# A sparse-attention and gated feed-forward kernel: unit 1's neighbour keys moved to where their transposes have landed, and part of its small copies given to ScalarE

## Chip, cores, metric

One core of a Trainium2 chip (the kernels ran on different chips, with the kernel before beside each). The metric is the device time of one execution in microseconds (us); each kernel's number is the median of its runs. Engines are named as in the profile: PE (matmul), PEld (weight load), DVE (VectorE), ACT (ScalarE), POOL (GpSimd), SP (SyncE).

## The reference, cut to what matters

```python
# attention, q,k,v: (4, 8, 768, 64) f32; block 32, window 16
k_sum = k.reshape(B,H,24,32,64).max(axis=3)       # a key per block: maximum over its 32 keys
v_sum = v.reshape(B,H,24,32,64).mean(axis=3)      # a value per block
# softmax over [local keys with |i-j| < 16] and [24 block keys, + log 32], times [v ; v_sum]
# then, on x = attention output as (3072, 512):
ffn = (gelu(x @ w_gate) * (x @ w_val)) @ w_out    # 512 -> 1536 -> 512
out = x + sigmoid(x @ w_res) * ffn
```

## The kernel before

The work is cut into eight units: unit u is half of batch u // 2, 384 tokens. While PE does the feed-forward of unit u, the attention of unit u + 1 is threaded in between. For one unit PE does twelve "columns" (line 398: four matmuls for the gate, g, and four for the value, vv), then in the tail scores (s, L330), residual gates (r, L416), the output matmuls (f, L432), attention outputs (ao, L362) and transposes (xp, L381). Each engine works in order through its own list of instructions: in the trace of before, the product gvT of column 9 could have run at about 66.03 us and ran at 67.73, behind work that waited for a DMA.

Unit 1 is special: it prepares batch 1, whose first use comes with unit 2. For each pair of heads a tile kW holds 64 own keys a row tile, their 16 neighbours on either side, and the 24 block keys; own keys of pairs 2 and 3 arrive by transposing DMAs. The value tile vext is loaded in even rows of tiles only; the odd ones are copied ("spread") from them, and block means are broadcast into rows 96 to 127.

```python
ps_mm = ...tile_pool(name="ps_mm", bufs=4, space=PSUM)   # results of matmuls; g, vv, r, f share four banks
...
def fo_end(gvT, fo, g, vv):
    nc.scalar.activation(ge[:], g[:, 0:TU], AF.Gelu)          # ACT; frees g's bank
    nc.vector.tensor_mul(gvT[:, fo, :], ge[:], vv[:, 0:TU])   # DVE; frees vv's bank
...
def k_rest(kw, copy=nc.vector.tensor_copy):
    nc.vector.tensor_max(km[:], ...)                          # L209
    nc.vector.tensor_reduce(out=ks..., in_=km[:], op=ALU.max) # L211, block keys
    copy(kw[:, 1:NT, 0:WIN], ...)                             # L213, neighbours before
    copy(kw[:, 0:NT - 1, POST:POST + WIN], ...)               # L214, neighbours after
    nc.vector.tensor_copy(kw[:, :, BLK0:BLK0 + NB], ...)      # L215, block keys
...
def v_spread(b, c0, c1, part):                                # part 0: L291, part 1: L294
def vsum_bc(b, hp, lo, hi, mul=...):                          # L300 for batches 0 and 1
...
# unit 1, after its columns 8 and 11
if u == 1 and fo in (8, FO - 1):
    k_rest(kW[1][2 if fo == 8 else 3])
...
# unit 1's tail
s_step(n, 0, nst); s_step(n, 1, nst, two=(AO, TT))            # scores, exponentials, masks
res_step(st, 0)
ffn_step(st, gvT, 0, 0, FO)
if u == 1:
    v_spread(1, 0, HT // 2, 0)
    v_spread(1, 0, HT // 2, 1)
    end_step(u, st, 0)                                        # two DVE ops on f
    vs = vsum_sum(1, *SS, last=True)                          # PE: block means
    vsum_out(1, vs, 0, H, nc.scalar.copy)
    for hp in range(NP):
        vsum_bc(1, hp, 0, HT)
res_step(st, 1)
if u == 1:
    ffn_step(st, gvT, 1, 0, 6)
# AO, TT, MM, SS name places in PSUM; rz: 1 / row sum, xn: normalised output
av_step(n, 0, nst, *AO); av_step(n, 1, nst, *TT)              # PE: ao; DVE: rz (L370), xn (L372)
s_step(n, 2, nst); s_step(n, 3, nst, two=(MM, MM), masked=False)
...                                                           # xp needs xn
```

The softmax here doesn't subtract the row's maximum and nothing guards it: scores larger than these inputs give would overflow.

Of the kernel before, what the change touches and what calls it, by code (L numbers as in the profile page):

```python
# [15 lines left out]
def kernel(  # L16
# [11 lines left out]
    nc = tc.nc  # L28
    B, H, S, D = q.shape
# [8 lines left out]
    FO = DFF // 128  # L38
    QT = 64
    NT = S // QT  # L40
    HT = NT // 2
# [3 lines left out]
    NP = H // 2  # L45
# [27 lines left out]
    kW = [[const.tile([128, NT, 128], BF16, name=f"kW{i}_{p}") for p in range(NP)] for i in range(2)]  # L73
# [30 lines left out]
    with tc.manual_schedule():  # L104

        def vext_consts(i):
            nc.vector.memset(vext[i][:, :, :, D:D + 1], 1.0)
            nc.vector.memset(vext[i][0:WIN, 0], 0.0)
            nc.vector.memset(vext[i][64:96, NT - 1], 0.0)
            nc.vector.memset(vext[i][64:64 + WIN, NT - 1, :, D:D + 1], 1.0)  # L110
# [57 lines left out]
        def gate(t):  # L168
            nc.gpsimd.tensor_copy(tick[:], t)
# [36 lines left out]
        def k_rest(kw, copy=nc.vector.tensor_copy):  # L206
            own = kw[:, :, OWN:OWN + QT].rearrange("d t (n w) -> d t n w", w=BLK)
            km = work.tile([128, NT, 2, BLK // 2], BF16, tag="km", name="km")
            nc.vector.tensor_max(km[:], own[:, :, :, 0:BLK // 2], own[:, :, :, BLK // 2:BLK])  # L209
            ks = work.tile([128, NB], BF16, tag="ks", name="ks")  # L210
            nc.vector.tensor_reduce(out=ks.rearrange("d (t n) -> d t n", n=2), in_=km[:],  # L211
                                    axis=mybir.AxisListType.X, op=ALU.max)
            copy(kw[:, 1:NT, 0:WIN], kw[:, 0:NT - 1, OWN + QT - WIN:OWN + QT])  # L213
            copy(kw[:, 0:NT - 1, POST:POST + WIN], kw[:, 1:NT, OWN:OWN + WIN])  # L214
            nc.vector.tensor_copy(kw[:, :, BLK0:BLK0 + NB], ks.unsqueeze(1).to_broadcast([128, NT, NB]))  # L215
# [68 lines left out]
            copy(vsum[b % 2][96:128, h0:h1, 0:D],  # L284
                 vs[96:128, h0 * D:h1 * D].rearrange("p (h d) -> p h d", d=D))

        def v_spread(b, c0, c1, part):

            V = vext[b % 2].rearrange("p (c e) h d -> p c e h d", e=2)
            if part == 0:  # L290
                nc.vector.tensor_copy(V[0:64, c0:c1, 1, :, 0:D], V[64:128, c0:c1, 0, :, 0:D])  # L291
            else:
                hi = min(c1, NC - 1)
                nc.vector.tensor_copy(V[64:96, c0:hi, 1, :, 0:D], V[0:32, c0 + 1:hi + 1, 0, :, 0:D])  # L294

        def vsum_bc(b, hp, lo, hi, mul=nc.vector.tensor_scalar_mul):
            dst = vext[b % 2][96:128, lo:hi, 2 * hp:2 * hp + 2, 0:D]
            if b < 2:
                src = vsum[b][96:128, 2 * hp:2 * hp + 2, 0:D]
                nc.vector.tensor_copy(dst, src.unsqueeze(1).to_broadcast([32, hi - lo, 2, D]))  # L300
            else:
                src = vsB[96:128, hp].rearrange("p (h d) -> p h d", d=D)
                mul(dst, src.unsqueeze(1).to_broadcast([32, hi - lo, 2, D]), 1.0 / BLK)
# [89 lines left out]
        def half_fo(st, w, fo, lo, hi, acc=None):  # L393
            fs = slice(fo * 128, (fo + 1) * 128)
            if acc is None:
                acc = ps_mm.tile([128, 512], F32, tag="mm", name="g" if w is w_gate else "vv")
            for ko in range(lo, hi):
                nc.tensor.matmul(acc[:, 0:TU], w[:, ko, fs], st["xT"][:, ko, :],  # L398
                                 start=(ko == 0), stop=(ko == KO - 1))
            return acc  # L400

        def fo_end(gvT, fo, g, vv):
            ge = work.tile([128, TU], F32, tag="ge", name="ge")
            nc.scalar.activation(ge[:], g[:, 0:TU], AF.Gelu)  # L404
            nc.vector.tensor_mul(gvT[:, fo, :], ge[:], vv[:, 0:TU])  # L405

        def fo_step(st, gvT, fo):
            g = half_fo(st, w_gate, fo, 0, KO)
            vv = half_fo(st, w_val, fo, 0, KO)
            fo_end(gvT, fo, g, vv)  # L410
# [16 lines left out]
        def ffn_step(st, gvT, sub, lo, hi, c0=0, c1=DM):  # L427
            ss = slice(sub * 128, (sub + 1) * 128)
            if lo == 0:
                st["f", sub] = ps_mm.tile([128, 512], F32, tag="mm", name="f")  # L430
            for fo in range(lo, hi):
                nc.tensor.matmul(st["f", sub][:, 0:c1 - c0], gvT[:, fo, ss], w_out[:, fo, c0:c1],  # L432
                                 start=(fo == 0), stop=(fo == FO - 1))
# [17 lines left out]
        def values_step(u, fo):  # L451

            b = u // 2 + 1
            if u in (2, 4) and fo >= FO - NP:
                block_sums(vT[b], fo - FO + NP)
            if u in (3, 5):
                if fo in (1, 3):
                    v_spread(b, 0, HT // 2, fo // 2)
                if 6 <= fo < 10:
                    vsum_bc(b, fo - 6, 0, HT, nc.scalar.mul)  # L460
            if u % 2 == 0 and u < NU - 1:
                if fo in (0, 1):
                    v_spread(b - 1, HT // 2, NC, fo)
                if 2 <= fo < 2 + NP:
                    vsum_bc(b - 1, fo - 2, HT, NT)
# [66 lines left out]
        for u in range(NU):  # L532
            b, half = u // 2, u % 2
# [16 lines left out]
            for fo in range(FO):  # L550
                if u == 0 and fo < 2:
                    for w, _, acc in firsts[2 * fo:2 * fo + 2]:
                        half_fo(st, w, fo, KO - 1, KO, acc)
                    fo_end(gvT, fo, firsts[2 * fo][2], firsts[2 * fo + 1][2])
                elif u > 3 and fo == 0:
                    fo_end(gvT, fo, firsts[0][2], firsts[1][2])
                elif u > 3 and fo == 1:
                    fo_end(gvT, fo, firsts[2][2], half_fo(st, w_val, fo, 0, KO))
                else:
                    fo_step(st, gvT, fo)  # L560
                values_step(u, fo)
                if u == 0 and fo == 4:
                    nc.vector.memset(vsT[:], 0.0)
                    load_rows(1)
                if u == 0 and fo == 6:
                    vext_consts(1)
                if u == 0 and fo == FO - 1:
                    kw_consts(1)
                    for c in range(NC + 1):
                        load_values(1, c)  # L570
                if u == 2 and fo == FO - 1:
                    gate(gvT[0:1, fo, 0:1])
                    load_rows(3)
                if half == 0 and 1 < nb < B and fo == 0:
                    vT[nb] = turn_values(nb)
                    turn_batch(nb, 0, NP - 1)
                if half == 1 and 1 < nb < B and fo == 0:
                    turn_batch(nb, NP - 1, NP)
                if half == 0 and 1 < nb < B and fo == FO - 1:
                    turn_sums()  # L580
                if half == 1 and 1 < nb < B and fo in (0, 2, 4, 11):
                    k_rest(kW[nb % 2][(0, 2, 4, 11).index(fo)], nc.scalar.copy)
                if u == 1 and fo == 6:
                    gate(gvT[0:1, fo, 0:1])
                    load_batch(2)
                if u == 1 and fo in (1, 2, 6, 7):
                    home = TT if fo % 2 else AO
                    if fo < 4:
                        k_step(nb, fo - 1, *home)
                    else:  # L590
                        q_step(q_sb[nb], nb, 0, S, fo - 6, *home)
                if u == 1 and fo in (8, FO - 1):
                    k_rest(kW[1][2 if fo == 8 else 3])
                if u == 0 and fo >= FO - 4:
                    k_later(kW[0][fo - FO + 4])
                if u == 0 and fo in (FO - 3, FO - 2):
                    for hp in range(2 * (fo - FO + 3), 2 * (fo - FO + 3) + 2):
                        q_step(qb, 0, TU, S, hp, *(TT if hp % 2 else AO))
# [41 lines left out]
            res_step(st, 0)  # L640
            ffn_step(st, gvT, 0, 0, FO)
            if u == 1:
                v_spread(1, 0, HT // 2, 0)
                v_spread(1, 0, HT // 2, 1)
                end_step(u, st, 0)
                vs = vsum_sum(1, *SS, last=True)
                vsum_out(1, vs, 0, H, nc.scalar.copy)
                for hp in range(NP):
                    vsum_bc(1, hp, 0, HT)
            res_step(st, 1)  # L650
            if u == 1:
                ffn_step(st, gvT, 1, 0, 6)
            av_step(n, 0, nst, *AO)
            av_step(n, 1, nst, *TT)
# [64 lines left out]
```

## Time and profile before

| | before |
|---|---|
| time, median of the first 3 runs | 258.7 us (258.38 to 258.93) |
| span of the profiled run, granted PE clock | 256.8 us, 1.000 |
| PE busy | 248.1 us (97%) |
| DVE, ACT, POOL busy | 67%, 55%, 39% |
| unit 1's first gate group to unit 2's first gate group, on PE | 51.42 to 84.48: 33.06 us |

PE is the engine to watch, and a change to DVE and ACT work can only take away its holes. A hole is read best from the distance between two starts on PE, compared with the distance of the same pair where nobody waits. The last row of the table, called U from here on, is such a distance: it lies inside one trace, so neither the start-up nor anything after unit 1 touches it. Its two ends in the timeline (start, duration, engine, line, operation):

```profile
51.42 0.81 PE L398 MATMUL g<-xT,w_gate 128*128 128x384 bf16 x4
...
84.48 0.81 PE L398 MATMUL g<-xT,w_gate 128*128 128x384 bf16 x4
```

The lines inside it are in the prediction.

### The profile page before, as it was taken

The page shows a single profiled execution, that of the slowest core. Times are in us where ns is not written, and L with a number is a line of the kernel's source. Part 1 is how long each engine was busy: PE and PEld are TensorE (multiplying, and loading weights), DVE is VectorE, ACT ScalarE, POOL GpSimd, SP SyncE. Part 2 cuts the span into 40 slices and gives each one's busy share as a digit, 9 for nine tenths or more (in the row PEclk, how much of TensorE's full clock was granted, in tenths as well). Part 3 has the DMA queues.
Part 4 walks back from the last instruction along what each step waited for, and adds up shares of the span by engine and source line. Part 5 has one row for each costly group of instructions (what it writes and reads, how often), then busy time and mean ns, then how long its engine had stood idle before and what let it go on. Part 6 is the DMA issues. An engine that isn't in the chain of part 4 may idle for free.

```text
span 256.8 us, 5742 instructions
## 1 busy us (share of the span) xinstructions
PE 248.1 (97%) x2223; PEld 139.1 (54%) x2249; DVE 173.2 (67%) x402; ACT 140.0 (55%) x247; POOL 101.3 (39%) x139
## 2 busy tenths in 40 slices
PE   7889999999999999999999999999999999999994
PEld 2546555566545565555554565555554655556543
DVE  5856866595598868669659769679568854664424
ACT  4855369455645636665983536455883537453310
POOL 7996543795589931986660100020001000010000
PEclk9999999999999999999999999999999999999999
DMA  7999999999999999999994975552003200130012
GB/s 154 154 153 194 198 202 201 145 198 131 135 151 166 176 144 153 146 186 203 156 138 88 162 127 95 68 134 68 0 3 88 84 0 1 33 138 3 0 41 82
DMA packets 117898, 30.15 MB, mean 117 GB/s; under 512 B 104816, under 2 KB 115504, under 8 KB 117872
## 3 DMA queue, kind: packets, MB, share of 16 engines
q0 software_dynamic: 86640, 19.11, 84.8%
q1 hardware_dynamic: 31232, 10.69, 25.2%
q8 instruction: 17, 0.28, 0.5%
q14 instruction: 9, 0.07, 0.1%
HBM read 32.51 MB, written 6.29 MB: 151 GB/s over the span
## 4 chain that ended last, share of the span: by engine, by line
PE 82%; DMA 6%; DVE 4%; POOL 3%; issue 2%; SPq 1%; ACT 1%; POOLq 0%; ACTq 0%; DVEq 0%
PE f L432 22%; PE vv L398 20%; PE g L398 19%; PE r L416 8%; DMA kW<-k_sb 4%; PE ao L362 3%; PE gv L548 3%; PE s L330 2%; DMA vext<-in_v_dram 2%; PE xp L381 1%; POOL vext L100 1%; DVE th L437 1%; DVE o L439 1%; PE vs L279 1%; SPq L251 1%
## 5 line engine op out<-in xcount | busy, mean ns | idle before, releaser
L398 PE MATMUL vv<-xT,w_val 128*128 128x384 bf16 x364 | 74.5, 326 | 0.5 <-DVE gvT L405 0.5
L404 ACT ACTIVATE ge<-g 128x384 f32<-128x384 f32 x87 | 42.7, 490 | 52.7 <-PE g L398 27.0
L398 PE MATMUL g<-xT,w_gate 128*128 128x384 bf16 x348 | 71.3, 326 | 0.1
L405 DVE TENSOR_TENSOR gvT<-ge,vv 128x384 bf16<-128x384 f32 x91 | 49.5, 551 | 30.1 <-PE vv L398 25.2
L432 PE MATMUL f<-w_out,gvT 128*128 128x512 bf16 (+2 forms) x298 | 66.5, 362 | 0.8 <-issue 0.2
L398 PEld LDWEIGHTS <-w_val 128*128 128x128 bf16 x368 | 35.9, 98 | 24.6 <-issue 0.7
L398 PEld LDWEIGHTS <-w_gate 128*128 128x128 bf16 x352 | 34.1, 98 | 22.5 <-issue 0.3
L432 PEld LDWEIGHTS <-gvT 128*128 128x128 bf16 x312 | 28.3, 98 | 28.2
L443 POOL DMA_DIRECT2D out_dram<-o x12 | 6.5, 545 | 90.5 <-DVE rz L370 75.6
L422 ACT ACTIVATE th<-r 128x512 f32<-128x512 f32 x24 | 14.2, 601 | 23.7 <-PE r L416 23.7
L437 DVE SCALAR_TENSOR_TENSOR th<-th,f 128x512 f32<-128x512 f32 (+2 forms) x26 | 16.7, 642 | 12.3 <-PE f L432 8.5
L175 POOL DMA_DIRECT2D k_sb<-in_k_dram x24 | 19.7, 835 | 13.0 <-DMA w_out<-in_moe_w_out_dram 5.2
L416 PE MATMUL r<-w_res,xT 128*128 128x512 bf16 x88 | 24.0, 380 | 0.4
L100 POOL DMA_DIRECT2D vext<-in_v_dram x28 | 23.5, 877 | 1.2 <-PE vv L398 1.2
L347 DVE TENSOR_TENSOR P<-P,maskt 128x768 bf16<-128x768 bf16 x28 | 15.4, 556 | 8.8 <-ACT P L339 4.7
L175 POOL DMA_DIRECT2D q_sb<-in_q_dram x24 | 19.9, 856 | 2.3 <-DMA k_sb<-in_k_dram 1.8
L372 DVE TENSOR_TENSOR xn<-ao,rz 128x384 bf16<-128x384 f32 x32 | 17.9, 558 | 1.1
L383 ACT COPY xT<-xp 128x384 bf16<-128x384 bf16 x20 | 9.3, 481 | 16.5 <-PE xp L381 16.5
L439 DVE SCALAR_TENSOR_TENSOR o<-th,xn 128x512 f32<-128x512 f32 (+2 forms) x26 | 16.9, 651 | 0.9
L336 ACT ACTIVATE P<-s,bias_t 128x384 bf16<-128x384 f32 x32 | 16.7, 578 | 1.0 <-PE s L330 1.0
L339 ACT ACTIVATE P<-s,bias_t 128x768 bf16<-128x768 f32 x16 | 14.4, 900 | 3.7 <-PE s L330 3.5
L175 POOL DMA_DIRECT2D v_sb<-in_v_dram x16 | 13.1, 855 | 3.2 <-DMA q_sb<-in_q_dram 3.0
(102 smaller groups left out, 238.7 us busy)
## 6 DMA issues: line engine op xcount, KB each, us to landing
out_dram<-o POOLq DMA_DIRECT2D x12, 256.0 KB, 2.4
out_dram<-o SPq DMA_DIRECT2D x11, 256.0 KB, 4.4
vext<-in_v_dram POOLq DMA_DIRECT2D x20, 128.0 KB, 7.0
k_sb<-in_k_dram POOLq DMA_DIRECT2D x24, 96.0 KB, 7.8
q_sb<-in_q_dram POOLq DMA_DIRECT2D x24, 96.0 KB, 5.6
w_gate<-in_moe_w_gate_dram POOLq DMA_DIRECT2D x6, 256.0 KB, 8.1
w_val<-in_moe_w_val_dram POOLq DMA_DIRECT2D x6, 256.0 KB, 8.7
w_out<-in_moe_w_out_dram POOLq DMA_DIRECT2D x3, 512.0 KB, 15.1
```

The lines of the kernel that those rows point to most:

```text
L100: nc.gpsimd.dma_start(out=dst, in_=v[b, :, lo:hi, :].rearrange("h p d -> p h d"))
L175: nc.gpsimd.dma_start(out=sb[b][:, h // 2, :, h % 2 * D:h % 2 * D + D], in_=src[b, h].rearrange("(c p) d -> p c d", c=NC))
L336: nc.scalar.activation(P[:, hh].rearrange("p t q -> p (t q)"), s[hh][:, 0:TU], AF.Exp, scale=scale, bias=bias_t[:])
L347: nc.vector.tensor_mul(Pf, Pf, maskt.unsqueeze(1).to_broadcast([128, 2 * HT, QT]))
L372: nc.vector.tensor_mul(xn, ao[:, :, :, 0:D], rz.to_broadcast([128, NSUB, 2, D]))
L398: nc.tensor.matmul(acc[:, 0:TU], w[:, ko, fs], st["xT"][:, ko, :], start=(ko == 0), stop=(ko == KO - 1))
L404: nc.scalar.activation(ge[:], g[:, 0:TU], AF.Gelu)
L405: nc.vector.tensor_mul(gvT[:, fo, :], ge[:], vv[:, 0:TU])
L416: nc.tensor.matmul(r[:], st["xT"][:, ko, ss], w_res[:, ko, :], start=(ko == 0), stop=(ko == KO - 1))
L432: nc.tensor.matmul(st["f", sub][:, 0:c1 - c0], gvT[:, fo, ss], w_out[:, fo, c0:c1], start=(fo == 0), stop=(fo == FO - 1))
L437: nc.vector.scalar_tensor_tensor(th, th, 1.0, f[:, 0:c1 - c0], ALU.add, ALU.mult)
L439: nc.vector.scalar_tensor_tensor(o[:, 0:c1 - c0].rearrange("p (k d) -> p k d", d=128), th.rearrange("p (k d) -> p k d", d=128), 0.5, st["x ...
```

## The change

Its intent: take two late DVE chains off PE's path in unit 1. The keys of pair 2 are finished after column 11, when their DMA has landed, those of pair 3 after the masks; ACT takes the neighbour copies of pair 3, the second half of the spread, and two of the four broadcasts. So that ACT can do them, the broadcasts become multiplies by 1.0; those of units 0 and 2, which stay on DVE, change with them.

```diff
-        def v_spread(b, c0, c1, part):
+        def v_spread(b, c0, c1, part, copy=nc.vector.tensor_copy):
             if part == 0:
-                nc.vector.tensor_copy(V[0:64, ...], V[64:128, ...])
+                copy(V[0:64, ...], V[64:128, ...])
             else:                                   # likewise
 ...
         def vsum_bc(b, hp, lo, hi, mul=nc.vector.tensor_scalar_mul):
 ...
-                nc.vector.tensor_copy(dst, src.unsqueeze(1).to_broadcast([32, hi - lo, 2, D]))
+                mul(dst, src.unsqueeze(1).to_broadcast([32, hi - lo, 2, D]), 1.0)
 ...
-                if u == 1 and fo in (8, FO - 1):
-                    k_rest(kW[1][2 if fo == 8 else 3])
+                if u == 1 and fo == FO - 1:
+                    k_rest(kW[1][2])
 ...
             if u == 1:
+                k_rest(kW[1][3], nc.scalar.copy)
                 v_spread(1, 0, HT // 2, 0)
-                v_spread(1, 0, HT // 2, 1)
+                v_spread(1, 0, HT // 2, 1, nc.scalar.copy)
                 end_step(u, st, 0)
                 vs = vsum_sum(1, *SS, last=True)
                 vsum_out(1, vs, 0, H, nc.scalar.copy)
-                for hp in range(NP):
+                for hp in range(2):
                     vsum_bc(1, hp, 0, HT)
             res_step(st, 1)
             if u == 1:
+                for hp in range(2, NP):
+                    vsum_bc(1, hp, 0, HT, nc.scalar.mul)
                 ffn_step(st, gvT, 1, 0, 6)
```

More of the change, by code (lines that the diff above doesn't have):

```diff
@@ L285, in vsum_out @@
                  vs[96:128, h0 * D:h1 * D].rearrange("p (h d) -> p h d", d=D))
-        def v_spread(b, c0, c1, part):
+        def v_spread(b, c0, c1, part, copy=nc.vector.tensor_copy):
             V = vext[b % 2].rearrange("p (c e) h d -> p c e h d", e=2)
             if part == 0:
-                nc.vector.tensor_copy(V[0:64, c0:c1, 1, :, 0:D], V[64:128, c0:c1, 0, :, 0:D])
+                copy(V[0:64, c0:c1, 1, :, 0:D], V[64:128, c0:c1, 0, :, 0:D])
             else:
                 hi = min(c1, NC - 1)
-                nc.vector.tensor_copy(V[64:96, c0:hi, 1, :, 0:D], V[0:32, c0 + 1:hi + 1, 0, :, 0:D])
+                copy(V[64:96, c0:hi, 1, :, 0:D], V[0:32, c0 + 1:hi + 1, 0, :, 0:D])
         def vsum_bc(b, hp, lo, hi, mul=nc.vector.tensor_scalar_mul):
```

## The prediction

> **What bounds the kernel now.** I read the head of the page first, then the chain of waits, then the timeline of the stretch that the change edits. The page:
>
> ```profile
> PE 248.1 (97%) x2223; PEld 139.1 (54%) x2249; DVE 173.2 (67%) x402; ACT 140.0 (55%) x247; POOL 101.3 (39%) x139
> PE   7889999999999999999999999999999999999994
> PE 82%; DMA 6%; DVE 4%; POOL 3%; issue 2%; SPq 1%; ACT 1%; POOLq 0%; ACTq 0%; DVEq 0%
> ```
>
> PE is the bound: 248.1 of 256.8 us, at nine tenths or more from the fourth slice to the last but one. A change that moves only VectorE (DVE) and ScalarE (ACT) work can give back no more than PE's holes in the stretch where that work lies. In the chain of waits in order of time, unit 1 (about 51 to 84.5 us) is the place where other engines stand in the chain after start-up:
>
> ```profile
> 56.61 9.54 DMA kW<-k_sb
> ...
> 66.24 0.37 DVE km L209
> ...
> 67.73 0.55 DVE gvT L405
> 68.28 0.04 issue
> 68.32 0.81 PE vv L398 x4
> ...
> 76.42 1.79 DVE vext L300 x4
> 78.21 0.03 issue
> 78.25 0.21 DVE rz L370
> 78.45 0.02 issue
> 78.48 0.57 DVE xn L372
> 79.05 0.05 issue
> 79.09 0.34 PE xp L381 x3
> ```
>
> The reader is to see two separate detours. First, the maximum over pair 2's keys (km) waits until 66.2 us for a transposing DMA; DVE works in order, so the product gvT of an earlier column, which had nothing to do with that DMA, comes only at 67.73, and PE waits for the PSUM bank that it frees. Second, four broadcasts of block sums (L300) stand on DVE ahead of the normalisation (rz, xn), and PE waits for that. The timeline of all engines, at the same two places:
>
> ```profile
> 66.24 0.36 DVE L209 TENSOR_TENSOR km<-kW 128x384 bf16<-128x384 bf16 x1 [0.96 <-DMA kW<-k_sb]
> ...
> 68.32 0.81 PE L398 MATMUL vv<-xT,w_val 128*128 128x384 bf16 x4 [0.45 <-DVE gvT L405]
> ...
> 76.97 0.71 PEld L362 LDWEIGHTS <-P 128*64 128x64 bf16 x24 [0.42 <-issue]
> ...
> 77.15 0.65 PE L362 MATMUL ao<-vext,P 128*64 128x65 bf16 x24
> ...
> 78.12 0.90 ACT L339 ACTIVATE P<-s,bias_t 128x768 bf16<-128x768 f32 x1 [1.74 <-PE s L330]
> ```
>
> Columns are start, duration, engine, line, operation, and in brackets the idle time before it with what ended it.
>
> **PE's holes, counted.** Starts are better than the printed idle, since matmul ends are modelled.
> Hole A: groups of four 128x384 matmuls start every 0.65 us. Column 11's gate group starts at 67.06, so its value group was due at 67.71 and came at 68.32: 0.61 us.
> Hole B: the six f matmuls start at 75.59; at 2.59 us for twelve (70.39 to 72.98) they need 1.30, so ao was due at 76.89 and came at 77.15: 0.26 us.
> Hole C: the scores start at 77.73 and need 0.46 (69.06 to 69.52), then three f need 0.65, so xp was due at 78.84 and came at 79.09: 0.25 us.
> Sum 1.12 us. Cross-check with unit 2, which has the same work without these edits: from its last value group (99.43) to the next unit's first gate group (113.35) is 13.92 us. Unit 1's is 68.32 to 84.48, 16.16; less its seven block-sum matmuls (72.98 to 74.72, 1.74) it is 14.42, so the tail has 0.50 to give, and B plus C are 0.51.
>
> **The Trainium skill.** "ScalarE: Activation LUTs", section "What ACT_TABLE_LOAD costs", gives an ACTIVATE with immediate scale and bias as 186 ns plus 0.833 ns an element, with back-to-back ones overlapping by about 93 ns. The trace agrees: 768 elements (L303 on ACT) should take 826 ns and take 848; the 176-element key copies should take 333 and take 328 to 338. The same page, "Rules for kernel authors", sends plain multiplies to VectorE as the faster engine. The trace has the same operation at 848 ns on ACT and 360 on DVE, so each move costs more engine time than it frees and pays only where ACT is idle and DVE late. "VectorE: DVE Perf Modes", "The perf-mode tier table", puts copy and scalar-multiply in one tier; the trace has them at 364 (median of L300) and 360 ns, so the replacement of copies by multiplies by 1.0, which also touches units 0 and 2, is neutral. "Perfetto Trace Analysis", "Optimization Strategy", says to look for the gaps on the most-contended engine and what blocks there, which is how the three holes were found.
>
> **The change part by part.** The instruction order of the built program shows no change of order on PE, POOL or the DMA queue; only DVE and ACT move, with no added table load.
>
> 1. Pair 2's neighbour keys go from after column 8 to after column 11. That removes 1.5 us of DVE work (66.24 to 67.73) and the DMA wait from between the products of columns 8 and 9. gvT starts 0.92 us after its value group (63.81 to 64.73), so those of columns 9, 10 and 11 come at 66.03, 67.33 and 68.63, and the bank is free long before 67.71. Hole A goes: 0.61 us. The DMA had landed by 66.2, so the moved step, at about 69.2, does not wait.
>
> 2. DVE after column 11. Keys of pair 2: 69.2 to 70.65. The two masks (P is ready at 70.6 and, from ACT, 71.55): to about 72.1. Keys of pair 3 without the two copies (0.36, 0.55, 0.24, little overlap): to about 73.25; their DMA landed at about 70.85. First half of the spread 0.72: to 73.97. End step 1.44: to 75.4. Two broadcasts of about 0.45 instead of four: to 76.3. DVE was free for rz at 78.25 before; now it is at 76.3, while PE with hole A gone reaches ao at 77.15-0.26-0.61 = 76.28. The first broadcast, the one ao needs first, ends at about 75.85. Hole B goes: 0.26. Then rz follows ao by 0.43 (105.05 to 105.48 in unit 2), xn ends at about 77.5, and PE wants it at 76.28+0.58+0.46+0.65 = 77.97. Hole C goes: 0.25.
>
> 3. ACT takes on: two key copies, 0.33 each; the other half of the spread, 1536 elements, by the skill's formula 1.47 us (an estimate; no trace row has it); two broadcasts of 0.85. Sum 3.8 us. Its idle time there was 2.78 (before the block sums at 74.82), 0.39 and 1.74. In order: the first tanh starts at 71.43, unchanged, because ACT stays held by the table load that ends at 69.70. Copies at 71.94 and 72.17, spread 72.4 to 73.9. Block sums at 74.82-0.61 = 74.21: ACT is free, 0.3 to spare. Second tanh 75.18, broadcasts 75.7 to 77.4, then the exponentials of pair 2 at 77.4. They would be possible at s + 0.39 = 77.25. So ACT is 0.15 us late, but their readers are further on: the last of this chain is the copy of the second xT half, at 77.4+2.64 = 80.05, and PE's ao of pair 3 wants its bank at about 80.15. It just fits.
>
> Total: 0.61+0.26+0.25 = 1.12 us at most off PE, of which I book about 1.0, because the ACT chain has only 0.1 us of slack at the end.
>
> After unit 1 PE is dense to the end, and its long waits on others are none, so the shift should arrive whole. One fixed time could bite: in unit 2 a DVE reduction waits for a transposed-values DMA until 101.65. If that stays put, the masks end at about 103.6, and PE, 1.1 us earlier, wants them at 103.95: still in time.
>
> **The rivals.**
> (a) ACT becomes the bound in the tail. For it: every moved operation is more than twice as slow there, and only 0.1 us is spare. Against it: 4.9 us of idle time in the stretch holds 3.8. If the spread takes 2 us rather than 1.47, or broadcasts have to wait for each other, the exponentials start at 78 as before and holes B and C come back at another instruction: gain 0.6, time 258.1.
> (b) The DVE chain is only moved: three groups still stand ahead of the broadcasts, and if DVE were late by 0.5 us more than I count, B and C stay: gain 0.6 to 0.8, time 257.9 to 258.1.
> (c) The gain is swallowed later, by DMAs whose times are set by the loads (DMA at nine tenths through unit 2). For it: PE starts unit 2 earlier, the loads do not. Against it: no PE wait on a DMA in the page after unit 1. It would make 258.5 to 258.7.
> (d) More gain than counted: removing DVE work could also tighten something that I take as fixed. The cross-check with unit 2 bounds the tail to 0.5, so not below 257.4 other than by scatter.
>
> **Range and chances.** Base 258.7 less 1.0 gives 257.7. The three runs before spread over 0.55 us, so 0.3 either way is scatter; (a) to (c) reach up to 258.5, (d) with scatter down to 257.1. Two per cent is 5.2 us, almost five times the sum of all holes, so outside it either way is left one chance in a hundred each: 0.01, 0.98, 0.01.
>
> **What would show it.** Step 1: km for pair 2 after column 11's gvT with no DMA wait, and value group 11 0.65 us after gate group 11. Step 2: ao directly 1.30 us after the six f, xp without a gap, rz at about 76.7. Step 3: the new spread row on ACT at about 1.47 us, exponentials of pair 2 at 77.3 to 77.5. The sum: unit 2's first gate group at 83.4 to 83.6 (before 84.48), and the span 1.0 shorter. Wrong would be: a PE wait named after ACT's vext or xT rows in the tail, or unit 2 starting a full microsecond earlier while the span stays.

## The result

The changed kernel took 258.01 us (median of 6, 257.46 to 259.20) against 258.68 us for the kernel before (6 runs, 258.26 to 258.93). The ratio of fast runs is 0.9979, with a 95% interval of 0.9956 to 1.0002. A ratio is the mean time of one kernel's fast runs over that of the other's of the same rounds, so it is not quite the ratio of the medians. Executions over 1.5% slower than the fastest of the same kernel are left out of the means. By time alone the first result is the same within 2% and does not even settle the sign. The trace does.

The head of the page of the changed kernel: busy shares, then the shares of the chain that ended last.

```profile
PE 249.0 (97%) x2249; PEld 138.9 (54%) x2249; DVE 172.2 (67%) x397; ACT 143.5 (56%) x252; POOL 101.2 (40%) x139
PE 92%; POOL 3%; DMA 2%; DVE 1%; issue 1%; ACT 0%; POOLq 0%; DVEq 0%
```

The chain was 82% PE and is now 92%: the DMA and DVE pieces of unit 1 have left it. (This trace has 26 PE records more than the earlier one, 2249 against 2223, though the programs have equal numbers of matmuls; PE's busy sums of the two should not be subtracted.) The chain of waits of the changed kernel in the same stretch (start, duration, what):

```profile
67.37 0.65 PE g L398 x4
68.02 0.65 PE vv L398 x4
68.67 0.46 PE s L330 x24
...
75.29 1.29 PE f L432 x6
76.58 0.50 PE ao L362 x24
77.08 0.46 PE s L330 x24
77.54 0.75 PE f L432 x3
78.29 0.17 PE xp L381 x3
```

In this view a PE piece starts where the one before it ends, and ends of matmuls are modelled; the starts used below are the timeline's, which are up to 0.17 us earlier. Nothing but PE stands there: vv follows g by 0.65 us, and ao and xp follow without anyone between. In the timeline of the changed kernel, the rows that answer to km, the broadcasts, rz and the exponentials of before:

```profile
69.25 0.35 DVE L209 TENSOR_TENSOR km<-kW 128x384 bf16<-128x384 bf16 x1
...
72.67 1.47 ACT L294 COPY vext<-vext 32x1536 bf16<-32x1536 bf16 x1
...
75.62 0.76 DVE L300 TENSOR_SCALAR vext<-vsum 32x768 bf16<-32x768 bf16 x2
...
75.94 1.59 ACT L300 ACTIVATE vext<-vsum 32x768 bf16<-32x768 bf16 x2
...
76.93 0.20 DVE L370 RECIPROCAL rz<-ao 128x6 f32<-128x6 f32 x1 [0.55 <-PE ao L362]
...
77.56 0.90 ACT L339 ACTIVATE P<-s,bias_t 128x768 bf16<-128x768 f32 x1
```

The key maximum of pair 2 no longer waits for a DMA; DVE is now waiting for PE at rz (0.55 us), where PE waited for DVE before; and ACT goes from its broadcasts into the exponentials without idle time. The first gate group of unit 2 starts at 83.51 instead of 84.48, although unit 1 began 0.14 us later (51.56): U is 31.95 us, 1.11 less than 33.06. Its ends:

```profile
51.56 0.81 PE L398 MATMUL g<-xT,w_gate 128*128 128x384 bf16 x4
...
83.51 0.81 PE L398 MATMUL g<-xT,w_gate 128*128 128x384 bf16 x4
```

### The profile page after: what moved, and what is told of

Same layout as the page of the kernel before. It is cut to its first block, busy times and chain, and to the rows that moved or that the text cites. A ratio compares the mean times of both kernels' runs of the same rounds, so it can differ in the third digit from the quotient of the medians.

```text
span 255.6 us, 5768 instructions
## 1 busy us (share of the span) xinstructions
PE 249.0 (97%) x2249; PEld 138.9 (54%) x2249; DVE 172.2 (67%) x397; ACT 143.5 (56%) x252; POOL 101.2 (40%) x139
## 4 chain that ended last, share of the span: by engine, by line
PE 92%; POOL 3%; DMA 2%; DVE 1%; issue 1%; ACT 0%; POOLq 0%; DVEq 0%
PE f L432 24%; PE vv L398 23%; PE g L398 22%; PE r L416 9%; PE ao L362 4%; PE gv L548 3%; PE s L330 2%; DMA vext<-in_v_dram 2%; PE xp L381 1%; POOL vext L100 1%; PE vs L279 1%; POOL k L91 1%; POOL qa L91 1%; PE gv L398 1%; PE tp L188 1%
## 5 line engine op out<-in xcount | busy, mean ns | idle before, releaser
L432 PE MATMUL f<-w_out,gvT 128*128 128x512 bf16 (+2 forms) x312 | 68.4, 363 | 0.0
L347 DVE TENSOR_TENSOR P<-P,maskt 128x768 bf16<-128x768 bf16 x28 | 15.5, 558 | 9.4 <-ACT P L339 4.7
```

What stands on the lines that cost most here:

```text
L347: nc.vector.tensor_mul(Pf, Pf, maskt.unsqueeze(1).to_broadcast([128, 2 * HT, QT]))
L432: nc.tensor.matmul(st["f", sub][:, 0:c1 - c0], gvT[:, fo, ss], w_out[:, fo, c0:c1], start=(fo == 0), stop=(fo == FO - 1))
```

## The experiments

All experiments gave correct results. "Before" was timed beside each: the ratios are to its runs, whose medians lie between 258.62 and 259.42, and not to the 258.68 of the first row. Each trace gives U and, from starts, the holes in it. The starts without a hole, from the changed kernel's trace: vv 0.65 us after its g, ao 1.39 after the first of the six f (75.12 to 76.51), xp 1.62 after ao (76.51 to 78.13). The table gives the holes, and the times of the runs (five timed rounds for each experiment, a single run in the last two rows):

| kernel | U | holes in U | time, median | ratio to before (95%) |
|---|---|---|---|---|
| before | 33.06 | vv 0.61, ao 0.17, xp 0.32 | 258.68 | |
| changed | 31.95 | none | 258.01 | 0.9979 (0.9956 to 1.0002) |
| again | 31.95 | none | 258.10 | 0.9958 (0.9928 to 0.9989) |
| move_only | 32.85 | ao 0.57, xp 0.32 | 259.81 | 1.0024 (0.9990 to 1.0058) |
| move_undone | 32.75 | vv 0.81 | 259.30 | 1.0008 (0.9973 to 1.0043) |
| bc_back | 31.94 | none | 258.24 | 0.9972 (0.9938 to 1.0006) |
| keys_back | 31.95 | none | 257.90 | 0.9966 (0.9943 to 0.9988) |
| spread_back | 32.82 | ao 0.45, xp 0.42 | 258.20 | 0.9994 (0.9964 to 1.0025) |
| keys_bc_back | 32.92 | ao 0.65, xp 0.32 | 258.54 | 0.9987 (0.9961 to 1.0013) |
| bc_all_act | 33.13 | at ao of pairs 2, 3: 1.18 | 259.04 | 1.0021 (0.9996 to 1.0046) |
| later_spread, later_spread2 | 31.95, 31.95 | none | 258.24, 258.30 | 0.9966 (0.9936 to 0.9996), 0.9967 (0.9931 to 1.0003) |
| keys_bc_late | 31.94 | none | 274.71 | |
| spread_late | 32.28 | ao 0.25, xp 0.08 | 274.29 | |

In every row U less the holes is 31.94 to 31.96: the holes account for all of it. The times are much noisier. In these traces unit 1 begins anywhere from 51.33 to 52.93 us, because the start-up and unit 0 take different times, which is more than the whole effect. The changed kernel and later_spread have two traces each; every other U rests on one.

### again: the changed kernel once more

> The changed kernel once more, unaltered, for a narrower interval and a second trace. Measure U: time on PE from unit 1's first gate group to unit 2's first gate group; before 33.06 us (51.42 to 84.48), after 31.95 (51.56 to 83.51). Theory (three holes closed, deterministic): U = 31.9 to 32.0 again, total 0.7 to 1.2 us under before. Rival (the gain is scatter): U anywhere between 32 and 33, total within 0.3 of before. The further 0.22 us that the first trace gained in unit 3 is expected to come and go, since no instruction there changed.

No edit. U was 31.95 again, and this time the ratio's interval lies below 1. The gain is not scatter.

### move_only: the new places, all on DVE

```diff
-                k_rest(kW[1][3], nc.scalar.copy)
+                k_rest(kW[1][3])
-                v_spread(1, 0, HT // 2, 1, nc.scalar.copy)
+                v_spread(1, 0, HT // 2, 1)
-                for hp in range(2):  ... (two broadcasts on ACT after res_step)
+                for hp in range(NP): vsum_bc(1, hp, 0, HT)
```

> The changed kernel with the ScalarE share given back: the keys of pairs 2 and 3 are done at the new places, but neighbour copies, both spread halves and all four broadcasts are on DVE. Theory: hole A (0.61) closes, but DVE has the same work to do after column 11 plus pair 2's keys, so the first broadcast ends at about 77.1 and rz starts at about 78.5; ao waits about 0.6 and xp about 0.55, so A's gain is handed back: U = 33.0 to 33.2, total within 0.3 of before. Rival (moving the keys is the gain, the ScalarE moves are decoration): U = 32.4, total 0.6 under before.

Rows of its timeline:

```profile
77.80 1.71 DVE L300 TENSOR_SCALAR vext<-vsum 32x768 bf16<-32x768 bf16 x4
...
78.45 0.65 PE L362 MATMUL ao<-vext,P 128*64 128x65 bf16 x24 [0.51 <-DVE vext L300]
...
79.55 0.20 DVE L370 RECIPROCAL rz<-ao 128x6 f32<-128x6 f32 x1
```

The 0.61 us at vv is gone, but ao now waits 0.57 and xp 0.32 for a DVE that has pair 2's keys to do as well. U is 32.85, a little better than I expected (33.0 to 33.2), and 0.21 under before. So moving the keys alone keeps a fifth of the gain: a wait removed at column 11 is met again a few microseconds later on the same engine.

### move_undone: ACT's share without the move

```diff
-                if u == 1 and fo == FO - 1:
+                if u == 1 and fo == 8:
                     k_rest(kW[1][2])
```

> The changed kernel with pair 2's keys put back after column 8; ScalarE keeps its share. Theory: hole A comes back whole and B and C stay closed: value group 11 about 1.2 us after gate group 11 instead of 0.65, U = 32.5 to 32.6, total 0.5 under before. Rival (holes are not additive, DVE catches up or PE loses the time again in the tail): U = 32.0 or 33.0.

Rows of its timeline:

```profile
67.18 0.36 DVE L209 TENSOR_TENSOR km<-kW 128x384 bf16<-128x384 bf16 x1 [1.10 <-DMA kW<-k_sb]
...
69.32 0.81 PE L398 MATMUL vv<-xT,w_val 128*128 128x384 bf16 x4 [0.64 <-DVE gvT L405]
```

The hole at vv is back, alone, at 0.81 us: U is 32.75, somewhat above the 32.5 to 32.6 that I expected. The size of this hole is not fixed. It follows the landing of a DMA: km starts 14.82 us after unit 1's first gate group in the trace of before (66.24 less 51.42) and 14.96 here (67.18 less 52.22). That accounts for 0.14 of the 0.20 excess; the block-key copy behind it took 0.58 us here. Giving back the move costs 0.80 us and giving back ACT's share costs 0.90 (move_only). Together that is more than the 1.11 that the change brings, so in these traces the two parts need each other: each closes holes that the other one alone would leave or open again.

### bc_back and keys_back: two of the three ACT moves given back, one at a time

```diff
# bc_back                                   # keys_back
-   for hp in range(2):                     -   k_rest(kW[1][3], nc.scalar.copy)
+   for hp in range(NP):                    +   k_rest(kW[1][3])
        vsum_bc(1, hp, 0, HT)
```

> The changed kernel with the two broadcasts of pairs 2 and 3 back on DVE. Theory from the trace of after: DVE then reaches rz at about 77.1 rather than 76.93, xn of pair 0 ends at about 77.9, and PE asks for it at 78.13, so nothing is lost: U = 31.9 to 32.05; ACT starts the exponentials of pair 2 at about 77.4 instead of 77.56. This part of the change would then buy nothing. Rival (each of the moves is needed): hole C comes back in part, U = 32.1 to 32.3.

> The changed kernel with the two neighbour copies of pair 3 back on DVE. Theory: 0.25 to 0.6 us more on DVE (these copies took 0.11 start to start, or up to 0.5 with the one after them stretched), first broadcast ends at 76.25 to 76.6 against PE at 76.51: U = 31.95 to 32.05, nothing or nearly nothing lost. Rival (each of the moves is needed): U over 32.2.

U was 31.94 and 31.95. In bc_back rz starts at 77.03 and xp at 77.89, which is 1.61 after ao. Neither of these two moves is needed in these traces. This is what the slack of DVE at rz (0.55 us in the changed kernel) had promised.

### spread_back: the third ACT move given back

```diff
-                v_spread(1, 0, HT // 2, 1, nc.scalar.copy)
+                v_spread(1, 0, HT // 2, 1)
```

> The changed kernel with the second half of the value spread back on DVE. Theory: the first broadcast on DVE ends 0.73 us later, at about 76.75, while PE wants ao at 76.51; ao waits about 0.25 and hole C stays closed (rz at about 77.2): U = 32.15 to 32.3. Rival (this part too is spare): U = 31.95.

U was 32.82, not 32.15 to 32.3: my expectation missed. Rows of its timeline:

```profile
77.07 0.97 DVE L300 TENSOR_SCALAR vext<-vsum 32x768 bf16<-32x768 bf16 x2
...
77.48 0.38 PE L362 MATMUL ao<-vext,P 128*64 128x65 bf16 x12 [0.39 <-DVE vext L300]
...
78.09 0.38 PE L362 MATMUL ao<-vext,P 128*64 128x65 bf16 x12 [0.23 <-ACT vext L300]
```

The reader is to see two waits. The first ao waits for the first broadcast, as expected though longer. The second ao waits for the second broadcast, which I had left out: the two DVE broadcasts take 0.97 us together, end at 78.04, and ao of pair 1 starts at 78.09. (The view names ACT's broadcast there, which ended at about the same moment, 78.05; this ao reads only the columns of pair 1, which DVE wrote, and the weight load that starts with it at 78.09 is put down to DVE's broadcast.) DVE was also later than the 0.72 us of spread explain: the first broadcast starts 1.43 us after the first f (75.64) against 0.50 in the changed kernel, 0.93 more.

### keys_bc_back: only the spread left on ACT

```diff
-                k_rest(kW[1][3], nc.scalar.copy)
+                k_rest(kW[1][3])
-                for hp in range(2):  ... (two broadcasts on ACT after res_step)
+                for hp in range(NP): vsum_bc(1, hp, 0, HT)
```

> The changed kernel with both the neighbour copies and the two broadcasts back on DVE, only half of the spread left on ACT. Theory: DVE reaches rz at 77.4 to 77.7, xn of pair 0 ends at 78.2 to 78.5 against PE's 78.13: a hole of 0.1 to 0.4, U = 32.05 to 32.35. Rival (half of the spread alone is the change): U = 31.95.

A larger miss: 32.92 where I expected 32.05 to 32.35. Each of the two had cost nothing alone; together 0.97 us. Rows of its timeline, DVE copies only:

```profile
73.89 0.53 DVE L213 COPY kW<-kW 128x176 bf16<-128x176 bf16 x1
74.00 0.46 DVE L214 COPY kW<-kW 128x176 bf16<-128x176 bf16 x1
74.39 0.21 DVE L215 COPY kW<-ks 128x288 bf16<-128x288 bf16 x1
74.63 1.10 DVE L291 COPY vext<-vext 64x1536 bf16<-64x1536 bf16 x1
```

The same copies take 0.20, 0.19 and 0.70 us elsewhere. Something stretches them. I had worked with their short or mean durations, and had seen unequal ones in the trace of before (0.20 to 0.56 at L213 to L215) without asking why.

### Why DVE copies stretch: a count, and two diagnostic kernels

Candidate: POOL, which issues DMAs by itself and was issuing batch 2's loads all through unit 1's tail. I counted the single DVE rows in all fourteen traces, by whether they overlap a row of POOL issuing a DMA, and called a row stretched if it was over 0.055 us above the least of its kind:

| DVE rows | no POOL issue beside it: stretched | POOL issue beside it: stretched |
|---|---|---|
| copies and multiplies by a constant (L213, L214, L215, L291, L294, L300, L303) | 0 of 319 | 150 of 381 |
| two-input multiplies and maxima (L347, L209) and the maximum-reduction (L211) | 0 of 381 | 0 of 314 |

For one form, L215, the range is 0.21 to 0.24 us without POOL beside it and 0.21 to 0.73 with. This is where a page would have helped me: the Trainium skill, "SBUF — State Buffer", section "Who interferes with whom", says that DVE in a two-port mode and GpSimd take a shared port pair from each other for a whole instruction, that copies and tensor_scalar can enter such modes, and that reductions cannot. The count agrees in which operations are hit; that the port pair is the reason, no run here shows. It is a count, not yet a cause, so two kernels moved POOL's loads of batch 2 to after unit 1 and left DVE's order as it was:

```diff
-                if u == 1 and fo == 6:
-                    gate(gvT[0:1, fo, 0:1])
-                    load_batch(2)
 ...
             end_step(u, st, 2)
+            if u == 1:
+                gate(nst["xT"][0:1, KO - 1, 0:1])
+                load_batch(2)
```

> keys_bc_back with one edit for diagnosis: POOL issues the loads of batch 2 only after unit 1 instead of from its column 6, so no issue of POOL overlaps DVE's copies in unit 1's tail (the kernel is meant to be slower later, where units 2 and 3 wait for these loads). DVE's order is the same. Theory (most of keys_bc_back's 0.97 us loss is DVE copies stretched while POOL issues DMAs): copies take their short durations (neighbour copies 0.19 to 0.20, spread 0.70), the first broadcast starts 0.5 to 0.6 us after the first of the six f matmuls instead of 1.27, and U = 31.95 to 32.1 instead of 32.92. Rival (the DVE work itself is too long): U stays near 32.9.

> spread_back with the same diagnostic edit. Theory: the stretched 0.2 us goes, the 0.72 us of real work stays; the first broadcast starts about 1.2 us after the first f instead of 1.43, ao of pair 0 waits about 0.2 and ao of pair 1 about 0.2 more for its own broadcast: U = 32.3 to 32.6 instead of 32.82. Rival (everything lost in spread_back was stretching): U = 31.95.

The same four rows in keys_bc_late:

```profile
73.67 0.20 DVE L213 COPY kW<-kW 128x176 bf16<-128x176 bf16 x1
73.78 0.20 DVE L214 COPY kW<-kW 128x176 bf16<-128x176 bf16 x1
73.89 0.22 DVE L215 COPY kW<-ks 128x288 bf16<-128x288 bf16 x1
74.15 0.70 DVE L291 COPY vext<-vext 64x1536 bf16<-64x1536 bf16 x1
```

U fell from 32.92 to 31.94: all of keys_bc_back's loss was stretching. In spread_back it fell from 32.82 to 32.28 (just under the 32.3 to 32.6 expected), so 0.54 us of that loss was stretching and 0.33 is real work on DVE. Both kernels are some 15 us slower in all, as meant: the distance from unit 2's first gate group to unit 3's is 45 us instead of 28.9, since batch 2 arrives late. The edit also takes the transfers themselves out of unit 1's tail (45 GB/s from 73 to 79 us against 156 in keys_bc_back), so these two runs alone do not part POOL's issuing from DMA traffic. The traces do: counted over all of them, 113 copies and constant multiplies had no POOL issue beside them while DMAs moved at 100 GB/s or more, and none of the 113 was stretched. Both ran once, in an unknown state; their matmul groups in unit 1 start every 0.65 us, as in the other traces, so U compares.

This bears on the kernel before, too, by an estimate that no run of it tests. From the first of its four broadcasts to rz it took 1.82 us (76.42 to 78.25); the same four took 1.22 in keys_bc_late, and the first one 0.37 instead of 0.67. That is 0.60 and 0.30 us, enough for all of the 0.32 at xp and of the 0.17 at ao. From km of pair 2 to the end of its block-key copy it took 1.57 us against 1.30, so 0.27 of the 0.61 at vv. About 0.76 of the 1.10 us of holes would then be stretching beside POOL's issues. In move_only, too, the four broadcasts took 1.71 us, against 1.19 in keys_bc_late. Whether issuing those loads at another time, early enough for unit 2, would have brought as much as the change is open.

### bc_all_act: ACT overloaded on purpose

```diff
                 for hp in range(2):
-                    vsum_bc(1, hp, 0, HT)
+                    vsum_bc(1, hp, 0, HT, nc.scalar.mul)
```

> The changed kernel with all four broadcasts on ACT, none on DVE: overloads ACT on purpose by 1.6 us. Theory of a nearly full ACT (0.1 us spare): exponentials of pair 2 start at about 79.0 instead of 77.56, the copies of xT that free the banks for ao of pairs 2 and 3 end at about 81.2 and 81.7, while PE wants them at 80.07: PE waits about 1.1 us there, U = 33.0 to 33.2, all of the gain gone. Rival (ACT has slack that I do not see, as its busy share of 56% suggests): U under 32.3.

Rows of its timeline:

```profile
78.85 0.90 ACT L339 ACTIVATE P<-s,bias_t 128x768 bf16<-128x768 f32 x1
...
81.11 0.76 PE L362 MATMUL ao<-vext,P 128*64 128x65 bf16 x24 [0.93 <-ACT xT L383]
```

U is 33.13, as expected, all of the gain gone and 0.07 more. Counted from unit 1's start the exponentials come 1.24 us later, and PE waits where predicted, for ACT's copies of xT. With an overall share of 56% ACT looks free, but in this stretch it is full: adding 1.6 us costs PE 1.18.

### later_spread: a try at a better kernel

```diff
-                if fo in (1, 3):
-                    v_spread(b, 0, HT // 2, fo // 2)
+                if fo in (1, 5):
+                    v_spread(b, 0, HT // 2, fo // 4)
```

> An attempt at a version that beats both: the changed kernel with one further edit, in units 3 and 5 the second half of the value spread goes from after column 3 to after column 5, so that DVE has a free column between two loaded ones. Reason: over ten traces the time from unit 3's first gate group to unit 4's was 28.36 (no hole) to 28.98 us, mean about 0.2 above the least, and in the long ones DVE's copies around columns 1 to 4 were stretched and gvT late. Theory: this distance is 28.36 to 28.40 in every trace, U of unit 1 stays 31.95, total 0.1 to 0.3 under the changed kernel, so 0.9 to 1.3 under before. Rival (the holes of unit 3 come from ACT's broadcasts in columns 6 to 9): the distance still varies from 28.36 to 29.

> The same kernel as later_spread, for a second trace: 28.36 to 28.40 again from unit 3 to unit 4, U = 31.95.

Unit 3's distance (first gate group to the next unit's) is 28.58 in the trace of before, 28.37 in that of the changed kernel, and between 28.36 and 28.98 over the ten traces of kernels that share this code and keep their loads early. Both traces of later_spread have 28.37. But four of those ten had 28.36 or 28.37 as well, so two good traces are not proof, and the medians (258.24 and 258.30) are no better than the changed kernel's 258.01 and 258.10. The two ratios put it 0.3% under before, with one interval that just reaches over 1; whether it beats the changed kernel stays open.

## Why the prediction was right

The predicted 257.7 us in 257.1 to 258.5 contains the 258.01 measured. That alone says little, since the six runs spread from 257.46 to 259.20 and the interval of the ratio includes 1; the steps, read in the trace, are the evidence. By its own steps:

- **Step 1, hole A, 0.61 us: right.** vv follows g by 0.65 us, and km does not wait. move_undone shows the part by itself, at 0.81: the size depends on when a DMA lands, which the prediction took as fixed.
- **Step 2, holes B and C, 0.26 and 0.25 us: the sum right, the split off.** PE needs 1.39 us from the first of six f to ao, not the 1.30 that six matmuls take, so B was 0.17; from ao to xp it needs 1.62, so C was 0.32. Together 0.49 against 0.51. The order of the chain was right, but a part of what the broadcasts cost was stretching, which the prediction did not know (see the estimate above). DVE's chain came as worked out: broadcasts at 75.62 (predicted 75.4, plus the 0.14 by which unit 1 began later), rz at 76.93 (76.71 plus 0.14, plus 0.08 for the slower step to ao).
- **Step 3, ACT: right.** The spread took 1.47 us, as estimated from the formula of "ScalarE: Activation LUTs", section "What ACT_TABLE_LOAD costs"; the exponentials began at 77.56 (77.4 plus 0.14). That ACT is nearly full (rival a) was right and harmless at this dose; bc_all_act shows the harm. Two readings there were off without effect: not every moved operation is over twice as slow on ACT (the neighbour copies took 0.35 and 0.36 us there, 0.20 on DVE), and in the trace of before such copies on ACT ran up to 340 ns, not 338.
- **Multiplies for copies, neutral: right.** Unit 2, which has the new multiplies too, takes 28.86 us from its first gate group to unit 3's before and 28.87 after.
- **Rival b, DVE late by 0.5 us more: did not happen in either trace of the changed kernel, but it is near.** spread_back and keys_bc_back are this rival, and their mechanism, stretching beside POOL's issues, was in no step of the prediction.
- **"PE is dense to the end": not quite.** Unit 3 had a hole of 0.22 us in the trace of before that I did not count. In that trace one block-key copy took 0.56 us instead of 0.24 and the products behind it were late; in the changed kernel's trace it took 0.24. So the traces differ by 0.22 us more, from 201.79 us between unit 1's first group and PE's end to 200.46, of which 1.11 is the change's.
- **The sum.** 1.12 predicted as the most, 1.11 in U, twice. I booked 1.0; the medians show 0.67 in the first rounds and 1.3 in the second, because the start-up moves by more than this.

## What to carry to other kernels

Work that waits for a DMA should not stand in an in-order engine's list ahead of work that frees the bound engine's buffers; but moving it pays only if its new place has slack, as move_only shows. Count slack in the stretch, not by the share of the span, and leave a margin: the changed kernel keeps 0.55 us on DVE at rz, while spread_back and keys_bc_back, which spend it, lost 0.87 and 0.97 us of the gain when copies were stretched. Effects under half a per cent are better read from a distance inside the trace than from the total.

## What the Trainium skill lacked or had wrong

- "SBUF — State Buffer", section "Who interferes with whom": the shared port pair is there, and I should have read it before predicting. It gives no size for short copies beside POOL's DMA issues: of 381 such DVE rows, 150 were stretched, L215 from 0.21 up to 0.73 us, L291 from 0.70 up to 1.14. It speaks of a full block for a whole instruction; 231 of the 381 overlapping rows were not stretched, so overlap with a row of POOL issuing does not by itself mean a block.
- The same section calls the exemption of tensor_tensor from descriptor writing inferred. The count supports it: 0 of 220 two-input rows (L347 and L209) were stretched beside POOL's issues.
